# A long convolution with a gated layer: the third transform stage with 64 moving columns, real and imaginary parts kept apart, mirrored places joined by sum and difference; one late tap moved

## The chip, the core and the metric

The kernel runs on one core of a Trainium2 chip. The core has TensorE (matrix products into PSUM; PE in the profile, with PEld for its weight loads), VectorE (DVE), ScalarE (ACT), GpSimd (POOL), and SyncE (SP), whose queue issues all transfers here. Each engine works through its own instructions in program order and waits on semaphores for the others. The metric is the device time of one execution in microseconds (us).

## What is computed

For eight sequences of 6400 places and 128 channels, a causal convolution with one filter as long as the sequence is followed by a small gated layer:

```python
Xf = rfft(x, n=2*S, axis=1); Hf = rfft(h, n=2*S, axis=0)
x = irfft(Xf * Hf, n=2*S, axis=1)[:, :S]
gate = sigmoid(sum_k conv_w[k] * shifted(x, K - 1 - k))      # K = 5 taps, per channel
out = (gate * (x @ w_val)) @ w_out
```

All numbers are float32, in and out. x is (8, 6400, 128), h is (6400, 128), w_val and w_out are 128 x 128.

## The kernel before

The long transform is done as matrix products. The 6400 places are a 100 x 64 grid (N1 = 100, N2 = 64), so a transform along the sequence becomes a product of length 100, one of length 64 with twiddle factors, a product with the filter's spectrum, and the same way back. For one batch there are four stages:

- The **forward** half (`Forward.half`): 16 calls of four channels pairs each; products of 50 rows by 100 columns, into PSUM, copied to `gy` (two copies of 400 elements, both on ScalarE). Its inputs `sd` are sums and differences that POOL makes from the loaded tiles `x` (two per call).
- **Second stage with the filter** (`Product`): products with `m2`, multiplied by the spectrum `h` on VectorE, added on POOL, back into `gy`.
- **Third stage** (`s3_quads`): 16 calls a batch, each for eight channels, from `gy` into `dt` (seen as `dv[p, n, c, d]`: place n of 64, part c real or imaginary, channel d).
- **Fourth stage** (`Chunk.s4`): from `dt` and the tables `m4` to the result of the convolution, in 13 chunks of four or five places n, followed by the taps, the value product (`project`), the sigmoid, the gate product on VectorE, the output product and the store.

Work of different batches is laid over each other by the main loop at the end of the function `longconv_moe`. For each batch b a first inner loop runs 16 steps g: the third stage of batch b (`s3_quads(4 * g)`), and beside it the forward half of batch b + 1 (if there is one). I call these 16 steps the third stage of a batch. A second inner loop then runs the fourth stage of batch b beside the second stage of batch b + 1. Five chunks of the fourth stage (places 35 to 59, `late`) leave their taps, value product, sigmoid and gate for the 16 steps of the next batch: the list `steps` gives late chunk m its first two taps in step 2m, the others in step 2m + 1, value product, sigmoid and gate in step 2m + 2, and for the first three chunks the output product in step 2m + 4 and the store in 2m + 5. So steps 0 to 9 carry taps; steps 10 to 15 carry only the rest of the last late chunk and a chunk called HEAD.

`_Engines` keeps every instruction of an engine in program order, so an instruction that waits holds back all behind it on that engine.

**The third stage in detail** (lines 331 to 351). A call has 32 matmuls: four channels q, two halves c of the sum, four combinations of row half r and channel half k. Weights are slices of `gy` (64 by 64, or 64 by 50 for the second half c), the moving operand is a row of `r3_sb` with 128 columns: 64 places times real and imaginary part, interleaved. The two halves c add up in PSUM (start at c == 0, stop at c == 1). A float32 matmul is two matmul instructions and two weight loads. The result lies in two single PSUM banks (`single()`, of four) and is copied to `dt` by two copies of 512 elements, the first on ScalarE, the second on VectorE (on ScalarE in the last batch). The forward half writes into a pair of banks (`pair()`, of two pairs here).

**The taps** (lines 396 to 450). A chunk adds its result, weighted, to the cells of five neighbours. `first(4, ...)` on ScalarE initialises a cell (`init`); `more(j, ...)` on VectorE adds tap j. For chunks that are not late the fourth tap (j = 3) is made by `first(3, ...)` on ScalarE into a buffer `p_t` and added by POOL; for late chunks all of j = 0, 1, 2, 3 are `more` on VectorE.

Of the kernel before, what the change touches and what calls it, by code (L numbers as in the profile page):

```python
# [16 lines left out]
C = 128  # L17
N1 = 100
# [35 lines left out]
def _constants():  # L54
    k1 = np.arange(N1, dtype=np.float64)
    n1 = np.arange(N1, dtype=np.float64)
    k2 = np.arange(N2, dtype=np.float64)
    n2 = np.arange(N2, dtype=np.float64)
    half = np.arange(2 * HP) % HP
    own = half < HR  # L60
    tau = 2.0 * np.pi
    a = tau * np.outer(half + 0.5, k1 + 0.25) / N1
    r1 = np.stack([np.cos(a) + np.sin(a), np.cos(a) - np.sin(a)], axis=1) * own[:, None, None]
    al = tau * (
        (k1[None, :, None] + 0.25) * n2[:, None, None] / N
        + np.outer(n2, k2)[:, None, :] / N2
        - (k1[None, :, None] + 0.25) / (2 * N1)
    )
# [7 lines left out]
    r3 = []  # L76
    for p in range(2):
        b = tau * np.outer(k2 + p / 2, n2) / N2
        c, d = np.cos(b), np.sin(b)
        g = 1 - 2 * p  # L80
        r3.append(np.stack([np.stack([c, -g * d], -1), np.stack([-d, -g * c], -1)], 1))
    r3 = np.concatenate(r3, axis=0)
    t = N2 * n1[None, :] + np.arange(N2 + 1)[:, None]
    sign = np.where(np.arange(2 * HP)[:, None] < HP, 1.0, 1 - 2 * (n1 % 2))
    m4 = np.cos(tau * (half[:, None, None] + 0.25) * t[None] / N) / N * own[:, None, None] * sign[:, None]
    m4 = np.concatenate([m4[:, :, ::2], m4[:, :, 1::2], -m4[:, :, 1::2]], axis=2)
# [25 lines left out]
def longconv_moe(ctx: ExitStack, tc: tile.TileContext, x, h, r1, m2, r3, m4, w64, out):  # L112
# [7 lines left out]
    psp = tc.tile_pool(name="psp", bufs=2, space=bass.MemoryType.PSUM)  # L120
    pairs = [ps2, psp.__enter__()]

    gy = cp.tile([128, C // 2, N1, 2], F32, name="gy")
    dt = cp.tile([128, N2 * 2 * C], F32, name="dt")
    dv = dt.rearrange("p (n c d) -> p n c d", c=2, d=C)
    gh = dt[:, : N1 * C].rearrange("p (d k t) -> p d k t", k=N1, t=2)
    m4_sb = cp.tile([128, N2 + 1, MW], F32, name="m4_sb")
    r1_sb = cp.tile([128, 2, N1], F32, name="r1_sb")
    r3_sb = cp.tile([128, 2, 2 * N2], F32, name="r3_sb")
    w_sb = cp.tile([C, NW], F32, name="w_sb")  # L130
    wc_sb = w_sb[:, 2 * C :]
    gl = cp.tile([128, N2 - LATE, N1], F32, name="gl")
# [78 lines left out]
    class Forward:  # L211
# [19 lines left out]
            e.tensor_tensor(out=sd[:, 0], in0=x[:, 0], in1=x[:, 1], op=ADD)  # L231
            self.load()

        def half(self):
            j = self.i
            self.i += 1
            sd = sd_sb[(j + self.o) % 3]
            pt = pair()
            for m in range(XG):
                for r, c in ((0, 0), (1, 1), (1, 0), (0, 1)):  # L240
                    rows = slice(r * HP, r * HP + HR)
                    nc.tensor.matmul(
                        pt[c * N2 : (c + 1) * N2, r, m * N1 : (m + 1) * N1],
                        lhsT=sd[rows, c, m, :],
                        rhs=r1_sb[rows, c, :],
                        start=True,
                        stop=True,
                    )
            v = pt[:, :, : XG * N1].rearrange("p r (d t k) -> p r d k t", t=2, k=N1)
            d0 = j * XG // 2  # L250
            return [
                lambda e, r=r: e(self.dst[:, r * C // 4 + d0 : r * C // 4 + d0 + XG // 2], v[:, r]) for r in range(2)
            ]

    def count(kb):
# [73 lines left out]
                e.tensor_tensor(out=self.u[:, c], in0=self.u[:, c], in1=self.t[:, 1 - c], op=op)  # L329

    def s3_quads(d0):
        pts = [single(), single()]
        for q in range(4):
            for c in range(2):
                for r, k in ((0, 0), (1, 0), (1, 1), (0, 1)):
                    d, o = k * HP + d0 + q, (r + k) % 2
                    m = HR if c else HP
                    nc.tensor.matmul(
                        pts[k][o * HP : o * HP + m, q * 2 * N2 : (q + 1) * 2 * N2],
                        lhsT=gy[r * HP : (r + 1) * HP, d // 2, c * HR : c * HR + m, d % 2],  # L340
                        rhs=r3_sb[r * HP : (r + 1) * HP, c, :],
                        start=c == 0,
                        stop=c == 1,
                    )
        return [
            lambda e, k=k: e(
                dv[:, :, :, k * HP + d0 : k * HP + d0 + 4].rearrange("p n c d -> p (n c) d"),
                pts[k].rearrange("p (d m) -> p m d", d=4),
            )
            for k in range(2)  # L350
        ]

    def m4v(n, c, k):
        v = m4_sb[:, N2 - n if c else n, :].rearrange("p (b m) -> p b m", m=HR)
        if c:
            return v[:, 1::-1, ::-1] if not k else v[:, ::-2, ::-1]
        return v[:, 0:2, :] if not k else v[:, ::2, :]

    def cells(x, n):

# [10 lines left out]
    class Chunk:  # L371
# [8 lines left out]
        def s4(self):  # L380
            a, n = self.ch
            pt = single()
            for q in range(n):
                for c in range(2):
                    for k in range(2):
                        o = slice(k * HP, (k + 1) * HP)
                        nc.tensor.matmul(
                            pt[o, q * N1 : (q + 1) * N1].rearrange("p (m b) -> p b m", b=2),
                            lhsT=dv[:, a + q, c, o],
                            rhs=m4v(a + q, c, k),  # L390
                            start=c == 0,
                            stop=c == 1,
                        )
# [34 lines left out]
        def taps(self, js=range(4)):  # L428
            a, n = self.ch
            if self.late and 0 in js:  # L430
                self.init()
            if a == HEAD[0]:
                for j in range(1, 4):
                    for i, o in cells(a + j, n - j):
# [77 lines left out]
    nc.sync.dma_start(r3_sb, r3)  # L512

    def m4_load(j):
        a = slice(CH * j, CH * j + CH)
# [27 lines left out]
    for b in range(B):  # L543
# [16 lines left out]
        for g in range(NS):  # L560
            e = s3_quads(4 * g)
            f = []
            if nxt:
                f = fx.half()
                fx.sums(nc.gpsimd)
            e[0](act)
            e[1](dve if nxt else act)
            for u in f:
                u(act)
            if b == 0:  # L570
                next(wgen, None)
                next(wgen, None)
# [107 lines left out]
```

## Time and profile before

| What | us |
|---|---|
| Median of three runs (lowest, highest) | 997.13 (994.02, 997.45) |
| The profiled execution's own time | 994.58 |
| Its span, from first to last instruction | 992.7 |
| Third stage of batch 2, to the first matmul of its fourth stage | 53.5 |
| Fourth stage of batch 2 | 59.5 |

The profile is of one execution. Its page gives the busy time of each engine, the chain of work that ended last, the groups of like instructions, and the DMA queues. A group's row reads: engine, operation, tile written and tiles read, shape, count, then total busy time and mean duration (ns) of one, then the idle time of the engine just before them and what ended it. Nearly all instructions are recorded at line 99, the helper that keeps program order, so groups are told apart by tiles and shapes: `pt<-r_sb,gy` is the third stage, `pt<-r_sb,sd` the forward half, `pt<-m_sb,dt` the fourth stage, `pt<-gy,m` the second, `dt<-pt` copies or taps, `sd<-x` POOL's sums. A row of the timeline reads: start, duration (of the merged instructions), engine, what, count, and in brackets the idle time before it with what ended it; "issue" is an engine that waited for nothing the profile shows. A row of the windows reads: stretch, its length, then each engine's busy time with its count, the clock granted to TensorE, the DMA engines' mean busy share and the rate in GB/s. Some matmul records can be missing from a trace.

### The profile page before, as it was taken

The page shows a single profiled execution, that of the slowest core. Times are in us where ns is not written, and L with a number is a line of the kernel's source. Part 1 is how long each engine was busy: PE and PEld are TensorE (multiplying, and loading weights), DVE is VectorE, ACT ScalarE, POOL GpSimd, SP SyncE. Part 2 cuts the span into 40 slices and gives each one's busy share as a digit, 9 for nine tenths or more (in the row PEclk, how much of TensorE's full clock was granted, in tenths as well). Part 3 has the DMA queues.
Part 4 walks back from the last instruction along what each step waited for, and adds up shares of the span by engine and source line. Part 5 has one row for each costly group of instructions (what it writes and reads, how often), then busy time and mean ns, then how long its engine had stood idle before and what let it go on. Part 6 is the DMA issues. An engine that isn't in the chain of part 4 may idle for free.

```text
span 992.7 us, 47023 instructions
## 1 busy us (share of the span) xinstructions
PE 936.5 (94%) x21360; PEld 818.4 (82%) x21360; DVE 685.2 (69%) x923; ACT 488.3 (49%) x932; POOL 544.6 (55%) x551
## 2 busy tenths in 40 slices
PE   7798879999999999999899999999999999999978
PEld 6698879888899879997799878998787888996854
DVE  4557437968299656967499665978489674976366
ACT  4522435536444554536444554536544464536656
POOL 5557534785177743786267842776367852760032
PEclk8999899999999999999999999999999999999989
DMA  7785545955387554855378563865478563850103
GB/s 242 249 293 206 187 168 202 277 135 192 100 265 199 172 194 138 246 167 174 121 245 221 151 200 122 259 167 183 139 242 222 142 206 110 265 144 24 42 23 112
DMA packets 96839, 177.35 MB, mean 179 GB/s; under 512 B 43392, under 2 KB 49792, under 8 KB 96640
## 3 DMA queue, kind: packets, MB, share of 16 engines
q1 hardware_dynamic: 96640, 174.34, 56.3%
q8 instruction: 168, 2.75, 1.1%
q14 instruction: 31, 0.25, 0.1%
HBM read 141.55 MB, written 32.77 MB: 176 GB/s over the span
## 4 chain that ended last, share of the span: by engine, by line
PE 88%; issue 4%; DMA 3%; DVE 2%; POOL 2%; ACT 1%; SPq 0%; DVEq 0%; POOLq 0%
PE pt L99 88%; DMA x<-xl 3%; DVE gl L99 1%; POOL sd L99 1%; ACT dt L99 1%; DVE dt L99 1%; POOL dt L99 0%; DMA x<-hl 0%; SPq L99 0%; POOL gl L99 0%; DVE gy L99 0%; DVE m_sb L99 0%; DVE sd L99 0%; ACT yl L99 0%; ACT gy L99 0%
## 5 line engine op out<-in xcount | busy, mean ns | idle before, releaser
L99 ACT COPY dt<-pt 128x512 f32<-128x512 f32 (+3 forms) x285 | 163.1, 582 | 251.9 <-PE pt L99 250.5
L99 PE MATMUL pt<-r_sb,gy 64*50 64x128 f32 (+1 forms) x8192 | 266.3, 274 | 21.4 <-issue 15.8
L99 POOL TENSOR_TENSOR gy<-gy,h 128x512 f32<-128x512 f32 (+1 forms) x182 | 221.1, 1240 | 117.9 <-PE pt L99 81.9
L99 PEld LDWEIGHTS pt<-r_sb,gy 64*50 64x50 f32 (+1 forms) x8192 | 235.8, 130 | 60.3 <-issue 26.6
L99 POOL TENSOR_TENSOR sd<-x 128x256 f32<-128x256 f32 x236 | 199.2, 869 | 143.6 <-issue 112.4
L99 PEld LDWEIGHTS pt<-m_sb,dt 128*64 128x64 f32 x4096 | 203.8, 137 | 30.0 <-issue 14.7
L99 PE MATMUL pt<-m_sb,dt 128*64 128x100 f32 x4096 | 205.6, 250 | 4.8 <-DVE dt L99 4.0
L99 PEld LDWEIGHTS pt<-gy,m 128*64 128x64 f32 x3008 | 192.7, 135 | 17.6 <-issue 5.3
L99 PE MATMUL pt<-gy,m 128*64 128x128 f32 x3008 | 199.7, 277 | 0.6 <-PE pt L99 0.5
L99 PE MATMUL pt<-r_sb,sd 50*64 50x100 f32 x4608 | 143.9, 258 | 23.6 <-issue 13.6
L99 DVE COPY dt<-pt 128x512 f32<-128x512 f32 (+1 forms) x120 | 81.4, 679 | 122.4 <-PE pt L99 109.9
L99 DVE TENSOR_TENSOR gy<-pt,h 128x1024 f32<-128x1024 f32 (+1 forms) x99 | 116.9, 1181 | 52.7 <-PE pt L99 26.5
L99 PEld LDWEIGHTS pt<-r_sb,sd 50*64 50x64 f32 x4608 | 128.2, 141 | 30.1 <-issue 16.7
L99 DVE SCALAR_TENSOR_TENSOR gl<-yl,w_sb,gl 128x500 f32<-128x500 f32 x147 | 127.5, 872 | 23.1 <-ACT gl L99 20.4
L99 DVE SCALAR_TENSOR_TENSOR dt<-pt,w_sb,dt 128x500 f32<-128x500 f32 (+7 forms) x216 | 132.6, 630 | 11.7 <-POOL dt L99 5.2
L99 ACT COPY gy<-pt 128x400 f32<-128x400 f32 x248 | 110.1, 496 | 45.8 <-PE pt L99 38.0
L99 PE MATMUL pt<-dt,w_sb 128*64 128x500 f32 (+2 forms) x480 | 126.2, 560 | 2.3 <-ACT dt L99 1.8
L99 DVE TENSOR_TENSOR h<-pt,h 128x1024 f32<-128x1024 f32 (+1 forms) x91 | 107.7, 1184 | 3.5
L99 ACT COPY yl<-pt 128x500 f32<-128x500 f32 (+1 forms) x89 | 51.0, 573 | 90.7 <-PE pt L99 90.6
L99 POOL TENSOR_TENSOR dt<-dt,p 128x500 f32<-128x500 f32 (+1 forms) x64 | 66.3, 1041 | 23.4 <-PE pt L99 12.7
L99 DVE TENSOR_TENSOR gl<-pt,gl 128x500 f32<-128x500 f32 (+1 forms) x48 | 31.5, 660 | 59.6 <-PE pt L99 33.2
L99 ACT ACTIVATE dt<-dt 128x500 f32<-128x500 f32 (+1 forms) x64 | 36.5, 571 | 66.5 <-POOL dt L99 66.1
(41 smaller groups left out, 588.2 us busy)
## 6 DMA issues: line engine op xcount, KB each, us to landing
m<-m SPq DMA_DIRECT2D x90, 512.0 KB, 5.3
h<-hd SPq DMA_DIRECT2D x84, 512.0 KB, 5.4
x<-xl SPq DMA_DIRECT2D x118, 256.0 KB, 2.9
out<-dt SPq DMA_DIRECT2D x56, 250.0 KB, 4.4
out<-yl SPq DMA_DIRECT2D x40, 250.0 KB, 2.6
m_sb<-m SPq DMA_DIRECT2D x13, 375.0 KB, 6.8
hd<-h SPq DMA_DIRECT2D x8, 512.0 KB, 4.7
m_sb<-m SPq DMA_DIRECT2D x6, 512.0 KB, 7.0
```

The lines of the kernel that those rows point to most:

```text
L99: return self._tc.keep_in_program_order(call(*args, **kwargs))
```

## The change

In the third stage the real and imaginary parts are no longer made for all 64 places. The two halves c of the sum are kept apart instead of added up in PSUM: each matmul has 64 moving columns (32 places for each of two parts), starts and stops by itself, and writes every second PSUM column. A call has as many matmuls as before. The results of places n and 64 - n are then the sum and the difference of the two halves, formed on the way out of PSUM. All weights are 64 by 64 now; the slices of the second half c run past their channel, so `gy` gets a zeroed tail, and the surplus rows meet zeros in `m4`. The third stage writes a pair of banks (`pair()`), the forward half two singles. The evacuation is four pieces: `keep` (ScalarE copies one half, 512 elements, to a scratch tile, half of `h_sb[HB - 1]`, used in turn), two `join`s (VectorE, sum and difference of PSUM and scratch, 496 elements each), and `ends` (ScalarE, two copies of 16 elements for places 0 and 32). In a step they come in the order keep, join, join, the forward half's two copies, ends. The upper places hold real and imaginary parts exchanged, which `m4` (with one row more) and `m4v` make good. The spectrum tile whose buffer is the scratch is loaded after the 16 steps. Apart from this, the fourth tap (j = 3) of late chunks is done as in the other chunks: `first(3, ...)` on ScalarE into `p_t`, added by POOL.

The changes in `_constants` (tables computed on the host's side) are left out, save the third stage's:

```diff
@@ _constants
     for p in range(2):
-        b = tau * np.outer(k2 + p / 2, n2) / N2
+        b = tau * np.outer(k2 + p / 2, n2[: N2 // 2]) / N2
         c, d = np.cos(b), np.sin(b)
-        g = 1 - 2 * p
-        r3.append(np.stack([np.stack([c, -g * d], -1), np.stack([-d, -g * c], -1)], 1))
+        q, r = -d, -d
+        q[:, 0], r[:, 0] = alt, -alt
+        r3.append(np.stack([np.concatenate([c, q], 1), np.concatenate([-c, r], 1)], 1))
...
@@ longconv_moe
-    gy = cp.tile([128, C // 2, N1, 2], F32, name="gy")
+    gyf = cp.tile([128, C * N1 + 2 * (HP - HR) + 4], F32, name="gy")
+    gy = gyf[:, : C * N1].rearrange("p (d k t) -> p d k t", k=N1, t=2)
+    nc.vector.memset(gyf[:, C * N1 :], 0.0)
...
-    m4_sb = cp.tile([128, N2 + 1, MW], F32, name="m4_sb")
+    m4_sb = cp.tile([128, N2 + 2, MW], F32, name="m4_sb")
...
-    r3_sb = cp.tile([128, 2, 2 * N2], F32, name="r3_sb")
+    r3_sb = cp.tile([128, 2, N2], F32, name="r3_sb")
...
@@ Forward.half
-        def half(self):
+        def half(self, pt=None):
...
-            pt = pair()
+            if pt is None:
+                pt = pair()
+                pt = [pt[:, 0], pt[:, 1]]
...
@@ s3_quads
-        pts = [single(), single()]
+        pt = pair()
         for q in range(4):
             for c in range(2):
                 for r, k in ((0, 0), (1, 0), (1, 1), (0, 1)):
                     d, o = k * HP + d0 + q, (r + k) % 2
-                    m = HR if c else HP
+                    w = d // 2 * 2 * N1 + c * 2 * HR + d % 2
+                    v = pt[o * HP : (o + 1) * HP, k, q * 2 * N2 : (q + 1) * 2 * N2].rearrange("p (b m) -> p b m", b=2)
                     nc.tensor.matmul(
-                        pts[k][o * HP : o * HP + m, q * 2 * N2 : (q + 1) * 2 * N2],
-                        lhsT=gy[r * HP : (r + 1) * HP, d // 2, c * HR : c * HR + m, d % 2],
+                        v[:, :, c::2],
+                        lhsT=gyf[r * HP : (r + 1) * HP, w : w + 2 * HP - 1 : 2],
                         rhs=r3_sb[r * HP : (r + 1) * HP, c, :],
-                        start=c == 0,
-                        stop=c == 1,
+                        start=True,
+                        stop=True,
                     )
-        return [
-            lambda e, k=k: e(
-                dv[:, :, :, k * HP + d0 : k * HP + d0 + 4].rearrange("p n c d -> p (n c) d"),
-                pts[k].rearrange("p (d m) -> p m d", d=4),
+        v = pt.rearrange("p k (d b m) -> p b m k d", b=2, m=N2)
+        a = d0 // 4 % 2 * 512
+        t = h_sb[HB - 1][:, a : a + 512]
+        o = dv.rearrange("p n c (k d) -> p (n c) k d", k=2)[:, :, :, d0 : d0 + 4]
+
+        def keep():
+            act(
+                t.rearrange("p (d m c) -> p d m c", m=N2 // 2, c=2)[:, :, :, ::-1],
+                pt.rearrange("p k (d b m c) -> p b (k d) m c", b=2, m=N2 // 2, c=2)[:, 1],
             )
-            for k in range(2)
-        ]
+
+        def join(op, n):
+            u = t.rearrange("p (k d m) -> p m k d", k=2, d=4)
+            nc.vector.tensor_tensor(out=n, in0=v[:, 0, 2:], in1=u[:, 2:], op=op)
+
+        def ends():
+            act(o[:, 0:2], v[:, 0, :2])
+            act(o[:, N2 : N2 + 2], v[:, 1, :2])
+
+        return keep, lambda: join(ADD, o[:, 2:N2]), lambda: join(ALU.subtract, o[:, : N2 + 1 : -1]), ends
...
@@ Chunk.taps
             if self.late and 0 in js:
                 self.init()
+                self.q = p_t[a // CH % 2]
+                self.first(3, self.q, self.p)
...
             for j in js:
-                if j < 3 or self.late:
+                if j < 3:
                     for i, o in cells(a + j, n):
                         self.more(j, o, self.p[:, i : i + o.shape[1]])
-            if self.late:
+            if 3 not in js:
                 return
             for i, o in cells(a + 3, n):
                 nc.gpsimd.tensor_tensor(out=o, in0=o, in1=self.q[:, i : i + o.shape[1]], op=ADD)
...
@@ main loop, the 16 steps
             if nxt:
-                f = fx.half()
+                f = fx.half([single(), single()])
                 fx.sums(nc.gpsimd)
-            e[0](act)
-            e[1](dve if nxt else act)
+            for u in e[:3]:
+                u()
             for u in f:
                 u(act)
+            e[3]()
...
-                else:
+                elif kb < M2B + HB - 1:
                     h_load(kb - M2B)
             for u in steps[g]:
                 u()
+        if nxt:
+            h_load(HB - 1)
```

More of the change, by code (lines that the diff above doesn't have):

```diff
@@ L76, in _constants @@
     r3 = []
+    alt = 1.0 - 2.0 * (k2 % 2)
     for p in range(2):
-        b = tau * np.outer(k2 + p / 2, n2) / N2
+        b = tau * np.outer(k2 + p / 2, n2[: N2 // 2]) / N2
         c, d = np.cos(b), np.sin(b)
-        g = 1 - 2 * p
-        r3.append(np.stack([np.stack([c, -g * d], -1), np.stack([-d, -g * c], -1)], 1))
+        q, r = -d, -d
+        q[:, 0], r[:, 0] = alt, -alt
+        r3.append(np.stack([np.concatenate([c, q], 1), np.concatenate([-c, r], 1)], 1))
     r3 = np.concatenate(r3, axis=0)
     t = N2 * n1[None, :] + np.arange(N2 + 1)[:, None]
-    sign = np.where(np.arange(2 * HP)[:, None] < HP, 1.0, 1 - 2 * (n1 % 2))
-    m4 = np.cos(tau * (half[:, None, None] + 0.25) * t[None] / N) / N * own[:, None, None] * sign[:, None]
-    m4 = np.concatenate([m4[:, :, ::2], m4[:, :, 1::2], -m4[:, :, 1::2]], axis=2)
+    up = np.arange(2 * HP)[:, None, None] >= HP
+    base = np.cos(tau * (half[:, None, None] + 0.25) * t[None] / N) / N * own[:, None, None]
+    flip = base * (1 - 2 * (n1 % 2))
+    m4 = np.where(up, flip, base)
+    m4[HP:, N2 // 2 + 1 :] *= -1
+    mid, odd = base[:, N2 // 2 : N2 // 2 + 1], flip[:, N2 // 2 : N2 // 2 + 1, ::-1]
+    m4[:, N2 // 2] = np.where(up, odd, mid)[:, 0]
+    m4 = np.concatenate([m4, np.where(up, mid, odd)], axis=1)
+    ev, od = m4[:, :, ::2], m4[:, :, 1::2]
+    late = ((np.arange(N2 + 2) > N2 // 2) & (np.arange(N2 + 2) <= N2))[None, :, None]
+    m4 = np.concatenate([np.where(late, od, ev), np.where(late, ev, od), np.where(late, -ev, -od)], axis=2)
     f = lambda v: np.ascontiguousarray(v.astype(np.float32))
@@ L242, in half @@
                     nc.tensor.matmul(
-                        pt[c * N2 : (c + 1) * N2, r, m * N1 : (m + 1) * N1],
+                        pt[r][c * N2 : (c + 1) * N2, m * N1 : (m + 1) * N1],
                         lhsT=sd[rows, c, m, :],
@@ L248, in half @@
                     )
-            v = pt[:, :, : XG * N1].rearrange("p r (d t k) -> p r d k t", t=2, k=N1)
+            v = [p[:, : XG * N1].rearrange("p (d t k) -> p d k t", t=2, k=N1) for p in pt]
             d0 = j * XG // 2
             return [
-                lambda e, r=r: e(self.dst[:, r * C // 4 + d0 : r * C // 4 + d0 + XG // 2], v[:, r]) for r in range(2)
+                lambda e, r=r: e(self.dst[:, r * C // 4 + d0 : r * C // 4 + d0 + XG // 2], v[r]) for r in range(2)
             ]
@@ L341, in s3_quads @@
                         rhs=r3_sb[r * HP : (r + 1) * HP, c, :],
-                        start=c == 0,
-                        stop=c == 1,
-                    )
-        return [
-            lambda e, k=k: e(
-                dv[:, :, :, k * HP + d0 : k * HP + d0 + 4].rearrange("p n c d -> p (n c) d"),
-                pts[k].rearrange("p (d m) -> p m d", d=4),
-            )
-            for k in range(2)
-        ]
-    def m4v(n, c, k):
[L354 to L357, printed above, removed]
+                        start=True,
@@ new lines, in join @@
+        def join(op, n):
[5 more added lines that the diff above has]
+        return keep, lambda: join(ADD, o[:, 2:N2]), lambda: join(ALU.subtract, o[:, : N2 + 1 : -1]), ends
+    def m4v(n, c, k):
+        e = N2 - n if c else n
+        if n == N2 // 2:
+            v = m4_sb[:, N2 + 1 if k else n]
+        else:
+            v = m4_sb[:, e]
+        v = v.rearrange("p (b m) -> p b m", m=HR)
+        w = v[:, :, ::-1] if c else v
+        if c == (e > N2 // 2):
+            return w[:, ::2] if k and n != N2 // 2 else w[:, 0:2]
+        return w[:, ::-2] if k and n != N2 // 2 else w[:, 1::-1]
@@ L388, in s4 @@
                             pt[o, q * N1 : (q + 1) * N1].rearrange("p (m b) -> p b m", b=2),
-                            lhsT=dv[:, a + q, c, o],
+                            lhsT=dv[:, a + q, 1 - c if a + q > N2 // 2 else c, o],
                             rhs=m4v(a + q, c, k),
@@ L514, in m4_load @@
     def m4_load(j):
-        a = slice(CH * j, CH * j + CH)
+        a = slice(CH * j, CH * j + CH + (j == 12))
         nc.sync.dma_start(m4_sb[:, a], m4.rearrange("k (n t) -> k n t", t=MW)[:, a])
```

## The prediction

> **What bounds the kernel now.** I read the page first, then the stretches of the stages (busy time of each engine in windows), then the timeline inside them, then the waits.
>
> ```profile
> PE 936.5 (94%) x21360; PEld 818.4 (82%) x21360; DVE 685.2 (69%) x923; ACT 488.3 (49%) x932; POOL 544.6 (55%) x551
> ...
> PE 88%; issue 4%; DMA 3%; DVE 2%; POOL 2%; ACT 1%; SPq 0%; DVEq 0%; POOLq 0%
> ...
> q8 instruction: 168, 2.75, 1.1%
> ```
>
> TensorE is busy for 94% and makes 88% of the chain that ended last, so a change that halves moving columns looks like a change on the path. That average hides the stages:
>
> ```profile
> core 0: us, PE busy (x) PEld busy (x) DVE busy (x) ACT busy (x) POOL busy (x), PEclk, DMA share, GB/s
> 98.30:153.00 54.70, 44.99 (x1519) 43.08 (x1523) 20.57 (x38) 22.24 (x46) 24.31 (x33) 0.91 0.49 161
> 326.50:380.00 53.50, 50.67 (x1573) 42.25 (x1572) 32.04 (x43) 30.29 (x61) 27.58 (x32) 1.00 0.51 160
> ...
> 890.90:931.90 41.00, 38.94 (x1061) 30.56 (x1060) 18.96 (x27) 24.67 (x47) 0.00 (x0) 1.00 0.07 23
> ```
>
> The rows are the third stage of batch 0, of batch 2 (I take it for 1 to 6) and of batch 7, which has no forward transform beside it. Only these change; the fourth stage between them keeps its work. How long does TensorE really need in one step?
>
> ```profile
> 826.29 1.98 PE L99 MATMUL pt<-r_sb,gy 64*64 64x128 f32 x64
> 828.09 0.87 PE L99 MATMUL pt<-r_sb,sd 50*64 50x100 f32 x32
> 828.78 1.93 PE L99 MATMUL pt<-r_sb,gy 64*64 64x128 f32 x64
> ...
> 890.85 5.47 PE L99 MATMUL pt<-r_sb,gy 64*64 64x128 f32 x192
> ```
>
> A step (64 matmul instructions of the third stage, 32 of the forward transform; each f32 matmul is two) goes from start to start in 828.78 - 826.29 = 2.49 us: 1.73 for the third stage (5.47 less a tail of 0.27, over three calls), 0.7 for the other. Sixteen steps are 39.8 us. Batch 0 has nothing else on TensorE and takes 54.7. Where the 15 us go:
>
> ```profile
> 138.76 0.97 PE L99 MATMUL pt<-r_sb,gy 64*64 64x128 f32 x27
> 142.92 0.92 PE L99 MATMUL pt<-r_sb,gy 64*50 64x128 f32 x12 [3.19 <-issue]
> ...
> PEld pt L99 <- issue: 9.5, 6, 3.4
> PE pt L99 <- issue: 8.2, 5, 3.2
> ```
>
> The first two rows are batch 0's timeline, the others its waits (us, times, longest). In the middle of a call TensorE stands still for 3.19 us and waits for no engine. The instruction queue of the page explains it: 168 packets for 2 x 21360 instructions, 254 in each. A step has 192, so the stage needs twelve packets, one every 54.7 / 12 = 4.6 us, and that, not the columns, is its length. I read it so: the next packet is asked for late, and under DMA load it takes some 4.6 us. The change leaves the count of instructions as it is.
>
> **The change part by part.**
>
> ```profile
> L99 PE MATMUL pt<-m_sb,dt 128*64 128x100 f32 x4096 | 205.6, 250 | 4.8 <-DVE dt L99 4.0 <-ACT dt L99 0.7
> ...
> L99 PE MATMUL pt<-r_sb,sd 50*64 50x100 f32 x4608 | 143.9, 258 | 23.6 <-issue 13.6 <-DVE sd L99 5.0 <-POOL sd L99 3.9
> ```
>
> Matmuls: same number, 64 columns for 128. Rounds of four go in 1.73 / 16 = 0.108 us at 128 columns and 0.7 / 8 = 0.087 at 100, so 64 columns should take 0.054 (in proportion) to 0.061 (on that line): some 0.93 us a call, 0.8 less, 13 us a stage. The other bound is no gain, if weight loads or the write of every second PSUM column limit it. The fourth stage writes every second column already (row one) and takes 250 ns at 100 columns where a contiguous write takes 258, so I take 0.93. The Trainium skill's "PSUM — Partial Sum Buffer", section Specifications, says that a non-contiguous pattern slows matmuls significantly; by it the call would stay at 1.73, which is rival 3.
>
> Evacuation, per step. It was one copy on ScalarE and one on VectorE. Now it is keep (512 elements, ScalarE), two joins (496 each, VectorE), then ends (two copies of 16, ScalarE).
>
> ```profile
> L99 ACT COPY dt<-pt 128x512 f32<-128x512 f32 x145 | 83.3, 586 | 149.8 <-PE pt L99 148.5 <-DMA x<-xl 1.4
> ...
> L99 ACT COPY gy<-pt 128x400 f32<-128x400 f32 x248 | 110.1, 496 | 45.8 <-PE pt L99 38.0
> ...
> L99 DVE COPY dt<-pt 128x512 f32<-128x512 f32 x112 | 76.9, 686 | 113.9 <-PE pt L99 109.9 <-DMA x<-xl 4.0
> ...
> L99 DVE TENSOR_TENSOR gl<-pt,gl 128x500 f32<-128x500 f32 x40 | 27.0, 678 | 45.7 <-PE pt L99 33.2 <-ACT gl L99 11.3
> ...
> 346.15 0.89 ACT L99 COPY gy<-pt 128x400 f32<-128x400 f32 x2
> ```
>
> VectorE: minus 0.69, plus 2 x 0.68. ScalarE: the copies of 400 and 512 give 0.8 ns an element over 0.175, so an end is 0.19; two copies of 0.496 take 0.89 together, so each overlaps its neighbour by 0.1, and both ends hold ScalarE for 0.18.
>
> The order costs more than the sums. Keep, joins and ends read the same two PSUM banks. Does a reader on ScalarE wait for a reader on VectorE? Before shows the pair the other way round, in the last batch:
>
> ```profile
> 937.72 0.68 ACT L99 ACTIVATE dt<-pt,w_sb 128x500 f32<-128x500 f32 x1
> ...
> 938.29 0.68 ACT L99 ACTIVATE p<-pt,w_sb 128x500 f32<-128x500 f32 x1
> ...
> 939.06 2.40 DVE L99 SCALAR_TENSOR_TENSOR dt<-pt,w_sb,dt 128x400 f32<-128x400 f32 x6 [0.38 <-ACT p L99]
> ...
> DVE dt L99 <- ACT p L99: 3.4, 3, 1.7
> ```
>
> VectorE's tap reads PSUM and dt, not p, yet starts 0.09 us after the ACTIVATE that fills p from the same bank, though dt was ready since 938.40. So readers of one bank go one after another, and I take 0.09 as the price of a hand-over. Then **ends waits for both joins, and behind ends, in order on ScalarE, stand the sigmoid, the initial tap, the new fourth tap, the store copy and the next keep**; the next joins, gate and taps on VectorE wait for those. A plain step is at least 0.59 + 0.09 + 0.68 + 0.68 + 0.09 + 0.18 = 2.3 us. The forward copies fit under the joins and cost nothing as long as TensorE is ahead.
>
> The fourth late tap: one of four taps goes from VectorE to an ACTIVATE and an add on POOL.
>
> ```profile
> L99 DVE SCALAR_TENSOR_TENSOR gl<-yl,w_sb,gl 128x500 f32<-128x500 f32 x140 | 123.7, 884 | 23.1 <-ACT gl L99 20.4
> ...
> L99 ACT ACTIVATE gl<-gl 128x500 f32<-128x500 f32 x40 | 25.1, 630 | 10.6 <-DVE gl L99 9.5 <-POOL gl L99 0.9
> ...
> L99 ACT ACTIVATE gl<-yl,w_sb 128x500 f32<-128x500 f32 x28 | 19.8, 708 | 0.0
> ...
> L99 POOL TENSOR_TENSOR gl<-gl,p 128x500 f32<-128x500 f32 x5 | 6.2, 1247 | 13.0 <-DVE gl L99 13.0
> ...
> L99 POOL TENSOR_TENSOR sd<-x 128x256 f32<-128x256 f32 x236 | 199.2, 869 | 143.6 <-issue 112.4
> ```
>
> A late chunk takes two steps. Even step, from the start of its keep: keep to 0.59, joins to 2.04, ends from 2.13, sigmoid of the chunk before 2.3 to 2.93, initial tap to 3.54, fourth tap (taken at 0.7) to 4.14. VectorE: gate 3.02 to 3.70, two taps to 5.47. Odd step: keep (from 4.04) is long done, joins 5.47 to 6.83, ends from 6.92, store copy 7.1 to 7.68, the next keep at 7.58; tap three to 7.71. **So 7.6 us a pair, 7.1 where nothing is stored.** POOL's add ends at 7.71 + 0.09 + 1.25 = 9.05, before the next sigmoid wants it (7.58 + 2.3): hidden. POOL's sums queued behind it are two steps ahead, and POOL has 4 x 0.87 + 1.25 = 4.7 us of work in 7.6. What the pair took before:
>
> ```profile
> 345.91 2.01 PE L99 MATMUL pt<-r_sb,gy 64*64 64x128 f32 x61
> ...
> 352.97 0.49 PE L99 MATMUL pt<-r_sb,gy 64*64 64x128 f32 x7
> ...
> 902.99 2.19 PE L99 MATMUL pt<-r_sb,gy 64*64 64x128 f32 x68
> ...
> 909.37 0.34 PE L99 MATMUL pt<-r_sb,gy 64*64 64x128 f32 x4
> ```
>
> 7.06 with the forward transform, 6.38 without. Pairs of the new stage: 6.5 (no gate yet), 7.1, 7.6, 7.6, 8.2 (the last late chunk has one short tap more), then for the steps with no taps 5.3 (gate at 3.70, joins and ends behind it), 5.1 and 4.7 (two plain steps, in one a sigmoid): 52.1, and 1.1 to the first keep, 53.2.
>
> Batch 7: 53.2, less 1.2 because its taps run without POOL beside them: 52 against 41.0, **plus 11**. There TensorE's 13 us are no help: its steps with no taps took 1.73 and take 2.3.
>
> Batches 1 to 6: 53.2, plus 1.0 for the first step (the forward copies stand before ends and wait for POOL's first sums), 54.2. Steps 10 to 15 count 15.1 in that; their 1152 instructions are 4.5 packets, up to 20 us at 4.6, but TensorE now comes there a step ahead; I add 1.0 of a possible 0 to 3. 55.2 against 53.5: plus 1.7, between -1 and +3.5, **six times: plus 10**.
>
> Batch 0: bound by packets before and after; the end gains the wait of the fourth stage for the last joins and ends (2.3 where the forward matmuls covered 0.7), less 0.8 of the last call: **plus 1** (-1 to +2).
>
> At nothing: one m4 row and 32 padding elements more; one h load moved behind the stage, on SP ahead of loads that are due later, wanted three steps later.
>
> Sum: 1 + 10 + 11 = 22 us on the profiled execution's 994.6 us (span 992.7): 1017. The median of the runs, 997.1, would give 1019.
>
> **Rivals.** 1. **Ends does not wait for the joins** (reads are ordered only where I saw it). Then ScalarE runs ahead and VectorE decides: 4 x 0.68 + 0.68 + 3 x 0.88 = 6.05 a pair, and 0.8 idle before the gate (add, sigmoid), 6.85 against 7.06; batches 1 to 6 gain 2 each, batch 7 loses 2: 985, faster. It decides as soon as ends starts within 0.2 us of the forward copies. For it: no data connects ends and joins. Against: the 0.38 us row.
> 2. **Packets do not bind the new stage**: then batch 0 goes by plain steps, 16 x 2.3 + 1 = 38, 18 less than forecast, and the 1.0 in each of six batches goes: 993, no change. For it: TensorE is idle in only 2.8 of the 53.5 us of batch 2. Against: the 3.19 us row, where TensorE had 2.49 us of work a step and will have 1.6. The Trainium skill stands on this side: "Runtime: NRT & Kernel Launch", section Instruction fetch mechanics, holds the refill in 16 KiB blocks to be hidden behind the issue of instructions.
> 3. **The matmuls gain nothing** (columns written two apart, or weight loads): 1.73 a call, TensorE is no step ahead, packets and chain add up, 2 to 3 us more in each of six: 1032.
> 4. **TensorE's time is the time**: 13 us in each of eight stages, 890. Against it: 32 joins of 0.68 alone are 21.8 us on VectorE where 11 went, and the packets.
>
> **How the numbers follow.** Forecast 0.70 (996 to 1031 from the bounds of the three terms), rival 1 0.10, rival 2 0.12, rival 3 0.06, rival 4 0.02. A measurement of this kernel tells some 0.5% (5 us) from no change. Faster is 1 and 4, 0.12; same is 2, 0.12; slower the rest, 0.76. The range takes the forecast and rival 2: 990 to 1033.
>
> **What would show it.** Right: ends starting 0.1 us behind the second join; VectorE idle before gates until ScalarE's gl; pairs of 7.1 to 7.6; the third stage of batch 7 near 52 us; batch 0 near 55 with TensorE idle "by issue"; a third-stage call in 0.9 to 1.0 us. Wrong: ends beside a join (rival 1); a call of 1.7 us (rival 3); batch 0 well under 50 (no packet limit); taps on VectorE far from 0.88.

## The result, and the profile after

The changed kernel takes 1063.31 us (median of 4 runs, 1059.4 to 1063.72) where the kernel before took 995.88 us beside it (994.02 to 997.45): a ratio of 1.0669, 95% interval 1.0635 to 1.0703. Slower, as forecast, but by 67 us and not by 22; the time lies 30 us above the range. Here and below a ratio compares runs in the chip's faster state only, with runs of the kernel before taken beside them.

The page of the changed kernel: busy time of each engine, the instruction queue, and the groups that answer to the evacuation.

```profile
PE 883.4 (84%) x21360; PEld 717.9 (68%) x21360; DVE 822.6 (78%) x1033; ACT 511.8 (48%) x1207; POOL 558.1 (53%) x586
...
q8 instruction: 168, 2.75, 1.1%
...
L109 DVE TENSOR_TENSOR dt<-pt,h 128x496 f32<-128x496 f32 x256 | 250.8, 1022 | 71.1 <-ACT h L109 59.1
```

The number of TensorE's instructions and of its packets is the same, and its busy time fell by 53 us. VectorE's rose by 137. The last row carries most of the result: **a join takes 1.02 us**, where the prediction took 0.68. 256 joins are 251 us of VectorE; at 0.68 they would be 174.

The windows of the changed kernel: busy time (and number) of PE, PEld, DVE, ACT, POOL, then granted clock, DMA share and GB/s. The rows are the third stage of batch 0, the third and the fourth stage of batch 2, and the third stage of batch 7.

```profile
core 0: us, PE busy (x) PEld busy (x) DVE busy (x) ACT busy (x) POOL busy (x), PEclk, DMA share, GB/s
96.70:150.28 53.58, 36.76 (x1536) 34.47 (x1537) 41.12 (x55) 25.96 (x79) 24.18 (x33) 0.84 0.48 156
331.90:391.85 59.95, 43.43 (x1574) 32.22 (x1573) 47.20 (x54) 35.16 (x100) 28.88 (x37) 0.96 0.41 133
391.85:453.60 61.75, 61.75 (x986) 52.58 (x987) 51.20 (x66) 25.81 (x49) 40.47 (x36) 0.96 0.71 209
938.30:995.94 57.64, 35.64 (x1064) 23.69 (x1061) 44.93 (x54) 22.27 (x67) 6.27 (x5) 0.78 0.05 16
```

Against the rows of before: batch 0 is 1 us shorter (54.70 to 53.58; the row of before stops 0.6 us short of the first fourth-stage matmul, up to which it is 55.3), batch 2 6.5 longer, batch 7 16.6 longer. The fourth stage, which the prediction left alone, is longer too. Its row before, in the same columns:

```profile
380.00:439.50 59.50, 59.50 (x992) 55.31 (x988) 51.33 (x67) 26.57 (x49) 40.47 (x36) 1.00 0.70 208
```

61.75 against 59.50, with the granted clock at 0.96 instead of 1.00. I cut the whole trace at the first matmul of each third and each fourth stage. The differences in span (1057.4 against 992.7):

| | forecast | changed kernel |
|---|---|---|
| third stage, batch 0 | +1 | -1.6 |
| third stages, batches 1 to 6 | +10 | +40.6 |
| third stage, batch 7 | +11 | +16.5 |
| eight fourth stages | 0 | +10.8 |
| ahead of the first third stage | 0 | -1.7 |

How a step goes shows in the timeline of batch 2, cut to the rows on the path (start, length, engine, operation, in square brackets the idle time before and what ended it):

```profile
341.10 0.60 ACT L109 COPY h<-pt 128x512 f32<-128x512 f32 x1
...
341.74 2.01 DVE L109 TENSOR_TENSOR dt<-pt,h 128x496 f32<-128x496 f32 x2 [0.15 <-ACT h L109]
...
343.78 0.25 ACT L109 COPY dt<-pt 128x16 f32<-128x16 f32 x2 [1.28 <-DVE dt L109]
343.92 0.63 ACT L109 ACTIVATE gl<-gl 128x500 f32<-128x500 f32 x1
...
344.58 0.68 DVE L109 TENSOR_TENSOR gl<-pt,gl 128x500 f32<-128x500 f32 x1 [0.83 <-ACT gl L109]
...
345.18 1.88 DVE L109 SCALAR_TENSOR_TENSOR gl<-yl,w_sb,gl 128x500 f32<-128x500 f32 x2
...
346.98 1.94 DVE L109 TENSOR_TENSOR dt<-pt,h 128x496 f32<-128x496 f32 x2
...
348.95 0.25 ACT L109 COPY dt<-pt 128x16 f32<-128x16 f32 x2 [1.94 <-DVE dt L109]
349.08 0.60 ACT L109 COPY h<-pt 128x512 f32<-128x512 f32 x1
```

This is the chain that the prediction wrote down: keep, two joins, ends within 0.1 us of the second join (341.74 + 2.01 = 343.75, then 343.78), the sigmoid behind ends, VectorE idle for 0.83 us until ScalarE has it, the gate, two taps, two joins, a tap that falls beside ends, the next keep. From keep to keep the pair takes 7.98 us where 7.1 was forecast (nothing is stored in this one): the two spans from joins to ends are 2.04 and 1.97 us instead of 1.45 each, 1.1 together, and the rest is 0.2 shorter.

### The profile page after: what moved, and what is told of

It reads as the page before. It is cut to its first block, busy times and chain, and to the rows that moved or that the text cites. A ratio compares the mean times of both kernels' runs of the same rounds, so it can differ in the third digit from the quotient of the medians.

```text
span 1057.4 us, 47726 instructions
## 1 busy us (share of the span) xinstructions
PE 883.4 (84%) x21360; PEld 717.9 (68%) x21360; DVE 822.6 (78%) x1033; ACT 511.8 (48%) x1207; POOL 558.1 (53%) x586
## 5 line engine op out<-in xcount | busy, mean ns | idle before, releaser
L109 DVE TENSOR_TENSOR dt<-pt,h 128x496 f32<-128x496 f32 x256 | 250.8, 1022 | 71.1 <-ACT h L109 59.1
L109 ACT COPY dt<-pt 128x16 f32<-128x16 f32 (+3 forms) x397 | 112.1, 319 | 286.1 <-DVE dt L109 183.1
L109 PEld LDWEIGHTS pt<-r_sb,gy 64*64 64x64 f32 x8192 | 149.9, 142 | 120.2 <-ACT dt L109 84.9
L109 PE MATMUL pt<-r_sb,gy 64*64 64x64 f32 x8192 | 168.4, 231 | 71.9 <-ACT dt L109 54.0
L109 PEld LDWEIGHTS pt<-gy,m 128*64 128x64 f32 x3008 | 182.0, 137 | 29.1 <-issue 24.9
L109 PE MATMUL pt<-r_sb,sd 50*64 50x100 f32 x4608 | 153.5, 259 | 54.7 <-issue 22.8
L109 POOL TENSOR_TENSOR sd<-x 128x256 f32<-128x256 f32 x236 | 170.1, 752 | 38.7 <-issue 15.9
L109 POOL TENSOR_TENSOR gl<-gl,p 128x500 f32<-128x500 f32 (+1 forms) x48 | 56.9, 1185 | 166.4 <-ACT yl L109 96.5
L109 DVE SCALAR_TENSOR_TENSOR dt<-pt,w_sb,dt 128x500 f32<-128x500 f32 (+7 forms) x216 | 132.6, 630 | 10.7 <-POOL dt L109 6.7
L109 PE MATMUL pt<-dt,w_sb 128*64 128x500 f32 (+2 forms) x480 | 114.5, 555 | 2.3 <-ACT dt L109 1.8
L109 ACT COPY h<-pt 128x512 f32<-128x512 f32 (+1 forms) x136 | 84.5, 622 | 35.6 <-PE pt L109 34.9
L109 DVE SCALAR_TENSOR_TENSOR gl<-yl,w_sb,gl 128x500 f32<-128x500 f32 (+1 forms) x112 | 89.9, 808 | 11.8 <-POOL sd L109 7.0
```

Source lines behind the costliest of these rows:

```text
L109: return self._tc.keep_in_program_order(call(*args, **kwargs))
```

## The experiments

### Is it the length of the join, and what makes it long?

In the changed kernel the scratch `t` lies in the order channel half, channel, place (k, d, m), and the joins walk it in the order place, half, channel: successive elements are 64 elements, 256 bytes, apart. The first experiment puts the scratch into the joins' own order. Keep still walks it in its old order, so now its writes have the gaps.

```diff
 keep:
-                t.rearrange("p (d m c) -> p d m c", m=N2 // 2, c=2)[:, :, :, ::-1],
+                t.rearrange("p (m c d) -> p d m c", m=N2 // 2, c=2)[:, :, :, ::-1],
 join:
-            u = t.rearrange("p (k d m) -> p m k d", k=2, d=4)
+            u = t.rearrange("p (m k d) -> p m k d", k=2, d=4)
```

> The changed kernel with the scratch laid out in the order in which the joins read it (places, then channels), so that a join's second input lies without gaps and keep writes with gaps instead. Theory (a join takes 1.02 us and not 0.68 because successive elements of its scratch input lie 64 elements apart): joins 0.67 to 0.70 us, keep no dearer than 0.70, a pair of steps with taps 7.1 to 7.4 us where it was 8.0, a step without taps 2.3 where it was 2.7; the whole 995 to 1025 us where the changed kernel has 1063. Rival (PSUM read in steps of 512 bytes beside any SBUF input, or the short runs of the output, make it slow): joins stay at 1.0 us, the whole at 1055 to 1070.

Measured: 1033.02 us, ratio 1.0415 (1.0362 to 1.0469). The groups of this run (busy time, mean ns of one, idle time before):

```profile
L109 DVE TENSOR_TENSOR dt<-pt,h 128x496 f32<-128x496 f32 x256 | 160.6, 669 | 127.1 <-ACT h L109 126.3
...
L109 ACT COPY h<-pt 128x512 f32<-128x512 f32 x128 | 150.4, 1175 | 18.2 <-PE pt L109 18.2
```

The joins fall from 1022 to 669 ns, as the theory said. It missed what keep would do: 1175 ns for 597, for the gaps have moved into ScalarE's writes, and VectorE now waits 126 us for keep (59 before). So the total came down by 30 us and not by the 38 and more that were expected.

The next kernel makes keep walk the scratch in the joins' order too. The gaps that are left are in the reads of PSUM.

```diff
 keep:
-                t.rearrange("p (m c d) -> p d m c", m=N2 // 2, c=2)[:, :, :, ::-1],
-                pt.rearrange("p k (d b m c) -> p b (k d) m c", b=2, m=N2 // 2, c=2)[:, 1],
+                t.rearrange("p (m c d) -> p m c d", m=N2 // 2, c=2)[:, :, ::-1],
+                pt.rearrange("p k (d b m c) -> p b m c (k d)", b=2, m=N2 // 2, c=2)[:, 1],
```

> The changed kernel with the scratch in the joins' order, as in the run e1, and keep also going through its elements in that order, so that neither touches SBUF with gaps between successive elements; PSUM alone is read in steps of 128 elements, as the copies before the change did. Theory (gaps in SBUF make the access slow, on either engine; steps in PSUM cost nothing): keep 0.58 to 0.62 us, joins 0.67, the stages as the forecast had them (about 55 us in batches 1 to 6, 52 in batch 7), the whole 1008 to 1025. Rival (the extra time sits in reordering 512 elements, wherever it is done): keep stays near 1.17, the whole near 1033.

Measured: 1005.3 us, ratio 1.0084 (1.0053 to 1.0116), a little under the expected 1008. Its groups, then its windows (third stage of batches 0 and 2, fourth stage of batch 2, third stage of batch 7):

```profile
L109 DVE TENSOR_TENSOR dt<-pt,h 128x496 f32<-128x496 f32 x256 | 160.2, 667 | 98.5 <-ACT h L109 98.5
...
L109 ACT COPY h<-pt 128x512 f32<-128x512 f32 x128 | 76.3, 596 | 38.0 <-PE pt L109 37.3 <-POOL sd L109 0.6
```

```profile
97.27:151.27 54.00, 36.15 (x1537) 34.03 (x1537) 30.12 (x55) 26.23 (x80) 23.96 (x33) 0.85 0.49 155
324.07:377.88 53.81, 42.75 (x1574) 31.49 (x1573) 37.48 (x54) 34.87 (x98) 30.58 (x37) 0.97 0.47 148
377.88:437.20 59.32, 59.32 (x985) 50.87 (x985) 51.20 (x66) 26.23 (x51) 40.44 (x36) 1.00 0.75 217
895.50:942.47 46.97, 30.90 (x1064) 21.46 (x1061) 34.27 (x54) 22.28 (x67) 6.25 (x5) 0.93 0.06 20
```

Two access patterns, with nothing else changed, take 58 us of the 67 away. Both instructions are now short (667 and 596 ns), though both read PSUM in steps of 128 elements: gaps in PSUM cost nothing here, gaps in the scratch, which lies in SBUF, cost 0.35 us a join or 0.58 us a keep. This is the kernel that the prediction priced, since its joins and its keep have the durations of the sum: against before its third stages are at -1.3 (batch 0), +7.9 (batches 1 to 6 together) and +5.9 us (batch 7), its fourth stages at +0.1.

The Trainium skill has this rule, and the prediction did not use it. Its page "SBUF — State Buffer", section "Door 1: The DMA port swizzle", says that SBUF gives full bandwidth within a line of 16 bytes and takes a penalty for each new line, so that float32 can be walked for free only in steps of up to four. The two rows of joins, 1022 and 667 ns, agree. The same passage says of PSUM, with lines of 8 bytes, that access with gaps slows matmuls; the matmuls of the changed kernel, which write every second column, show none of it (below).

### Is it the place of ends?

Ends reads the same two banks as the joins, and the prediction said that it waits for them and holds back all of ScalarE. The edit puts it right behind keep:

```diff
-            for u in e[:3]:
+            for u in (e[0], e[3], e[1], e[2]):
                 u()
             for u in f:
                 u(act)
-            e[3]()
```

> The changed kernel with ends issued right after keep, ahead of both joins, nothing else. Theory (readers of the same banks go one after another, and ends behind the joins holds ScalarE up, with the sigmoid, the initial taps and the next keep behind it): ScalarE no longer waits for VectorE in a step, a pair with taps goes by VectorE's own work, 4 x 0.95 + 0.68 + 3 x 0.82 = 6.9 us, where it was 8.0, and a step without taps by two joins, 1.95, or by the packets of instructions; the whole 1025 to 1045 us. Rival (VectorE's sum binds already, and the wait of ends costs nothing): the whole within 6 us of 1063.

Measured: 1033.95 us, ratio 1.0405 (1.0355 to 1.0456), with joins as long as in the changed kernel. The group of ends in the changed kernel, and then in this one:

```profile
L109 ACT COPY dt<-pt 128x16 f32<-128x16 f32 x256 | 31.7, 177 | 183.1 <-DVE dt L109 183.1
```

```profile
L109 ACT COPY dt<-pt 128x16 f32<-128x16 f32 x256 | 33.9, 195 | 0.0
```

ScalarE stood idle before ends for 183.1 us, all of it released by VectorE; here it does not wait at all, and the time falls by 29 us. The same edit on the kernel with short joins:

> The run e8 with ends issued right after keep, ahead of the joins. Theory (two separate costs, slow joins and the hold-up of ScalarE, so the gains add up): batches 1 to 6 at the packets' 50 to 53 us, batch 7 at 42 to 45, the whole 985 to 1003. Rival (they overlap, and once the joins are fast the order of ends is worth nothing): within 5 us of e8.

Measured: 1001.97 us (8 runs, 994.27 to 1012.66), ratio 1.0027 (1.0 to 1.0055): 3 us better than without it, which the two intervals do not separate. It is the best version of the change by its median, and it does not beat the kernel before. The total fits the theory and the rival alike; the stages tell more. In batch 7 the order is worth 4.5 us (46.94 to 42.44), as the theory said; batches 1 to 6 went from 55.0 to 54.4 on average, where 50 to 53 was expected, and the fourth stages lost 3.3 us in all, since two more of them began at half clock. Why so little? TensorE's waits (us in total, times, longest) in the changed kernel, then in this one:

```profile
PE pt L109 <- ACT dt L109: 55.8, 52, 3.1
PE pt L109 <- issue: 38.8, 35, 3.2
```

```profile
PE pt L109 <- issue: 64.5, 46, 3.2
PE pt L109 <- DVE dt L109: 22.8, 24, 2.7
```

In the changed kernel TensorE waits most for the evacuation, here for nothing that the profile shows, "issue". As the evacuation gets shorter, that wait takes its place.

### What bounds the third stage before: columns or instructions?

Two edits on the kernel before. Both halve the columns that TensorE has to stream; the first keeps the number of matmuls, the second halves it and keeps 128 columns in each (left out here: the copies of the first, which read its 64 columns twice, and start and stop of the second, both now True):

```diff
 half the columns:
-                        pts[k][o * HP : o * HP + m, q * 2 * N2 : (q + 1) * 2 * N2],
+                        pts[k][o * HP : o * HP + m, q * 2 * N2 : q * 2 * N2 + N2],
-                        rhs=r3_sb[r * HP : (r + 1) * HP, c, :],
+                        rhs=r3_sb[r * HP : (r + 1) * HP, c, :N2],
...
 half the instructions:
-            for c in range(2):
+            for c in range(1):
...
```

> The kernel before with 64 moving columns in the third stage and the copies as they were in size and number (each reads the 64 columns twice, so the output is not the reference's: half of the places of the third stage are left out and filled with the other half). The count of TensorE's instructions is unchanged. Theory (packets of instructions bind the third stage): batch 0's stage stays at 52 to 55 us, the whole at 970 to 995. Rival (TensorE's time is the time): 13 us less in each of eight stages, 890 to 905.

> The kernel before with only the first half of the sum in the third stage: 16 matmuls of 128 columns a call where it has 32, the copies unchanged (the second half of the sum is left out, so the output is not the reference's). The columns streamed are those of the run with half the columns, the instructions of a step 128 where there 192. Theory (packets): batch 0's stage 36 to 42 us, the whole 905 to 935, some 60 us below the run with half the columns. Rival (columns count, instructions do not): the same as the run with half the columns within 6 us.

Measured: 973.52 us with half the columns, ratio 0.9795 (0.9731 to 0.986); 914.16 us with half the instructions, ratio 0.9198 (0.9152 to 0.9245). The windows, third stage of batch 0 and of batch 7, for half the columns and then for half the instructions, with the instruction queue of the latter:

```profile
99.70:152.54 52.84, 36.98 (x1536) 35.07 (x1536) 20.82 (x39) 22.61 (x46) 24.20 (x33) 0.81 0.51 167
874.50:906.80 32.30, 27.46 (x1061) 19.14 (x1060) 18.99 (x27) 24.51 (x47) 0.00 (x0) 1.00 0.08 29
```

```profile
97.73:139.10 41.37, 32.71 (x1024) 31.09 (x1024) 21.60 (x39) 22.07 (x46) 24.39 (x33) 0.84 0.63 211
818.30:849.72 31.42, 27.09 (x550) 17.25 (x549) 19.00 (x27) 24.34 (x47) 0.00 (x0) 1.00 0.08 27
```

```profile
q8 instruction: 136, 2.23, 1.0%
```

In batch 0 (55.3 us before, cut in the same way), with DMA traffic beside it, half the columns give 2.4 us and half the instructions 13.9. In batch 7, with next to no traffic (DMA share 0.08), both give about the same, 8.7 and 9.6 us. TensorE's waits go with this: with half the columns, 13.3 us of them are by "issue" in batch 0 and none in batch 7, where 4.0 us are for VectorE and ScalarE. So beside the loads the third stage is bound by the arrival of TensorE's instructions: 32 packets fewer are four a stage, and 13.9 us for four packets is 3.5 us each. The DMA rows of the instruction queue, for batch 0 before and for batch 7 with half the columns:

```profile
q8 instruction: 12, 0.20, 1.4%
```

```profile
q8 instruction: 9, 0.15, 1.8%
```

1.4% of 16 engines for 54.7 us, over twelve packets, is 1.0 us each, and 1.8% for 32.3 us, over nine, is 1.0 as well: a packet travels no longer with the loads than without. In the trace of before, each of the five waits by "issue" in batch 0 ends 1.3 to 1.4 us behind the landing of a packet, so these waits are for packets that come late. What makes them late, no run here shows.

The change halves columns only. What it could win was therefore 2 to 3 us a stage in batches 0 to 6 (half the columns: 2.4 us in batch 0, 2.8 on average in the others) before anything was paid for the evacuation.

### The fourth late tap

In the changed kernel the move is undone; in the kernel before it is made alone, by the same lines the other way round:

```diff
 Chunk.taps, on the changed kernel:
                 self.init()
-                self.q = p_t[a // CH % 2]
-                self.first(3, self.q, self.p)
...
-                if j < 3:
+                if j < 3 or self.late:
...
-            if 3 not in js:
+            if self.late:
                 return
```

> The changed kernel with the fourth late tap back on VectorE. Theory (VectorE decides the steps with taps): each of five pairs in seven stages longer by 0.4 to 0.7 us, the whole 1073 to 1090. Rival (the tap's ACTIVATE on ScalarE, which is held up anyway, costs as much as it frees on VectorE): within 6 us of 1063.

> The kernel before with only the fourth late tap moved to ScalarE and POOL. Theory (before, TensorE and its packets set the length of the steps with taps, VectorE has room): no change, 989 to 1000, at most 1 us in any stage. Rival (the sigmoid waits for POOL's add, later than for the tap on VectorE): 0.5 us in each of 35 pairs, 1005 to 1015.

Measured: 1077.27 us, ratio 1.0801 (1.0752 to 1.085), 14 us worse than with the move; and 998.62 us, ratio 0.9997 (0.9968 to 1.0027), no difference. The move pays where VectorE is on the path, as it is with the long joins, and nothing where it is not.

### Why are the fourth stages longer?

The timeline of the changed kernel at the end of the third stage of batch 2: the last forward matmuls, the last joins, the last ends, and the first fourth-stage matmuls. Behind it TensorE's row of the kernel before at the same place.

```profile
389.57 0.40 PE L109 MATMUL pt<-r_sb,sd 50*64 50x100 f32 x6 [1.54 <-issue]
...
389.80 1.90 DVE L109 TENSOR_TENSOR dt<-pt,h 128x496 f32<-128x496 f32 x2 [0.80 <-ACT h L109]
...
391.73 0.25 ACT L109 COPY dt<-pt 128x16 f32<-128x16 f32 x2 [0.83 <-DVE dt L109]
...
391.85 2.93 PE L109 MATMUL pt<-m_sb,dt 128*64 128x100 f32 x32 [1.88 <-DVE dt L109]
```

```profile
380.01 1.67 PE L99 MATMUL pt<-m_sb,dt 128*64 128x100 f32 x31
```

TensorE stands still for 1.54 us by "issue", works for 0.40, stands still for another 1.88 us until the last joins and ends are through, and then its first 32 matmuls take 2.93 us where 31 took 1.67. To see whether the idle time makes them slow, four matmuls of constants by constants, into a bank that nobody reads, fill it:

```diff
         if nxt:
             h_load(HB - 1)
+        pt = single()
+        for q in range(4):
+            nc.tensor.matmul(
+                pt,
+                lhsT=r3_sb.rearrange("p c n -> p (c n)"),
+                rhs=m4_sb[:, :N2].rearrange("p n t -> p (n t)")[:, 512 * q : 512 * q + 512],
+                start=True,
+                stop=True,
+            )
```

> The changed kernel with four more f32 matmuls of 128x512 (constants by constants, into a bank that nobody reads) on TensorE behind the last third-stage call of each batch, in the 1.9 to 4.2 us in which it stood idle before the fourth stage. Theory: the 1 to 2.8 us by which the first 64 fourth-stage matmuls are later in the changed kernel's trace (9.2 to 10.7 us instead of 7.9) come from a clock that drops when TensorE idles; with the filler they take 7.9 to 8.2 us again, the fourth stages are 59.3 to 59.6 us (before: 59.5), and the total falls by 6 to 10 us, to 1053 to 1057. Rival: the fourth stages are longer because VectorE and ScalarE are behind by then; the filler changes nothing (1061 to 1065), or delays the stage by its own length (1068 and more).

Measured: 1055.76 us, ratio 1.0613 (1.0581 to 1.0645). The timeline at the place, and the windows of the third and fourth stage of batch 2:

```profile
390.35 3.70 PE L109 MATMUL pt<-m_sb,r_sb 128*128 128x512 f32 x8
393.98 1.59 PE L109 MATMUL pt<-m_sb,dt 128*64 128x100 f32 x32
```

```profile
332.57:393.98 61.41, 45.74 (x1582) 32.24 (x1580) 47.25 (x54) 35.23 (x100) 28.92 (x37) 1.00 0.42 132
393.98:453.40 59.42, 59.42 (x989) 52.25 (x988) 51.21 (x66) 25.70 (x47) 40.47 (x36) 1.00 0.74 218
```

The 32 matmuls are back at 1.59 us, and the fourth stage at 59.42 with the clock at 1.00; cut in the same way, the eight fourth stages fall from 486.5 to 473.6 us. None of them begins at half clock, while in the changed kernel the clock is down at the beginning of seven of the eight, or falls within 1 us of it. The total falls by less, since the third stages, at whose end the filler stands, are longer in this trace (483.6 us in all against 474.2). By the totals alone the two intervals overlap a little; the rows carry the verdict. The Trainium skill, "TensorE: Matmul & The Clock Gate", section "Part 1: The HAM clock gate", says that TensorE's clock is halved after an idle window of some 3.4 us, and that the windows run freely. 2.93 against 1.59 us is nearly a factor of two and agrees. The idle time agrees less. The windows of the changed kernel around the place, cut where its granted clock changes:

```profile
386.60:390.01 3.41, 1.82 (x84) 1.43 (x75) 2.61 (x4) 1.95 (x6) 0.00 (x0) 1.00 0.02 5
390.01:396.84 6.83, 5.00 (x46) 4.22 (x48) 1.69 (x2) 1.82 (x6) 0.10 (x1) 0.50 0.25 79
396.84:400.25 3.41, 3.41 (x60) 3.33 (x58) 1.76 (x2) 1.17 (x3) 0.00 (x0) 1.00 0.44 109
```

The clock fell at 390.01 us, 0.04 us into the idle time of 1.88 us, so it was not this one alone that brought it down. It stayed at half for 6.83 us, which is two times 3.41, and all changes of the clock in this trace are whole multiples of 3.41 us apart, as windows that run freely would have it. But no window without work was needed: in the 3.41 us before the fall TensorE was busy for 1.82.

> The changed kernel with the scratch in the joins' order and kept in that order, ends ahead of the joins, and the same filler. Theory: its trace without the filler lost 1.6 us in two of eight fourth stages, so the filler is worth 0 to 4 us there: 997 to 1002, not measurably under the kernel before, because the third stages of batches 1 to 6 stay at 53 to 56 us (twelve packets of some 4.5 us). Rival: the third stage is bound by its evacuation and not by packets, and the filler, with its 8 more instructions, is seen as nothing: 1002, or worse by its own 3.5 us in each batch, 1025.

On the best version the same filler is a miss: 1013.43 us, ratio 1.0195 (1.0155 to 1.0234), against 1001.97 without. There TensorE's idle time before a fourth stage was 0.1 to 2.4 us, the filler takes 3.7, and what it delays is more than the clock gives back: in the two traces the fourth stages gain 5.5 us in all and the third stages lose 14.7.

## Why the prediction was right or wrong

**The direction was right, the size was not, and the step that failed is the price of the join: "VectorE: minus 0.69, plus 2 x 0.68".** The 0.68 came from the row of the gate product (678 ns), whose SBUF operand has no gaps; the join's has one behind each element. It measured 1.02 us. The prediction gave this price no second bound, so the range could not hold it. What the missing 0.34 us did, the comparison with the kernel with short joins shows: 10.7 us in batch 7 (32 joins of 0.355 us are 11.4), 33 us in batches 1 to 6, and the loss of clock in the fourth stages.

**Batches 1 to 6** were forecast at 55.2 us. With joins as priced they are 55.0 on average (330.2 / 6); with joins of 1.02 us they are 60.5 (363.0 / 6). That 55.0 meets 55.2 is in part luck. With short joins the four pairs behind the first, which carry taps, take 7.0 to 7.7 us in batch 2, from keep to keep, and the sum has 7.1 to 8.2; the plain step takes some 2.1 and the sum has 2.3 (with long joins it takes 2.8). Against that the pair of steps 12 and 13 takes 6.2 to 10.2 us in batches 1 to 6, where the sum has 5.1 and batch 7 takes 4.6. In batch 2 TensorE waits there for 1.70 us by "issue". So the allowance of 1.0 us for packets was too small by about 2, which the shorter pairs and steps made up.

**Batch 7**, forecast at 52, is 57.64, and 46.97 with joins as priced. Here the sum was 5 us too high. Its plain steps of 2.3 us take 2.1, and its taps of 0.88 us, of which it took off 1.2 us in all, take 0.74, with no sums of POOL beside them. The two taps behind a gate take, in the kernel with short joins, in batch 2 and in batch 7:

```profile
335.79 2.30 DVE L109 SCALAR_TENSOR_TENSOR gl<-yl,w_sb,gl 128x500 f32<-128x500 f32 x2
...
905.86 1.51 DVE L109 SCALAR_TENSOR_TENSOR gl<-yl,w_sb,gl 128x500 f32<-128x500 f32 x2
```

Over a stage's sixteen taps that is 3.2 us less than in batch 2, and over 2 us less than at the price of 0.88. In the total the 5 us hid part of the error of the joins.

**Batch 0**, "bound by packets before and after", held: 53.58 us for the forecast 55. Half the columns left it at 52.84, half the instructions took it to 41.37. Rival 2 (packets do not bind) is refuted by that, and with it, for this kernel, the rule of the Trainium skill that the prediction set beside it ("Runtime: NRT & Kernel Launch", section Instruction fetch mechanics): here the refill is not hidden. The prediction's reading that a packet takes some 4.6 us under load held only in part: it is on its way for 1.0 us, with the loads as without, and eight packets at 4.6 us would make 37 us and not 41.

**Ends waiting for the joins** was right to 0.1 us, and rival 1 is refuted by 183.1 us of idle time. "The order costs more than the sums" was wrong, though, with joins as priced: without that order the short joins still give 1001.97 instead of 1005.3; TensorE's waits by "issue" are behind it. Its 29 us exist only beside the long joins.

**A call** goes in 0.9 us, as forecast; rival 3 (matmuls gain nothing) is refuted. In the third stage of batch 2 of the changed kernel:

```profile
358.69 1.19 PE L109 MATMUL pt<-r_sb,gy 64*64 64x64 f32 x64
...
360.55 1.19 PE L109 MATMUL pt<-r_sb,gy 64*64 64x64 f32 x64
```

1.19 less the tail of 0.27 is 0.92. Rival 4 fell with the rest: TensorE's time was not the time.

**The fourth stage at nothing** was wrong by 10.8 us. The prediction saw that the fourth stage now waits for the last joins and ends, and counted 1.6 us for it in batch 0; it did not ask what the idle time does to TensorE's clock. **The fourth tap** hidden on ScalarE and POOL was right.

What stays open: in which cases an idle time lowers the clock. In the changed kernel it fell in batch 2 behind a window of 3.41 us in which TensorE was busy for 1.82 us. In batch 5 it stayed up through an idle time of 3.64 us, which lies in two windows with 1.74 and 1.45 us of work. So the busy time of a window alone does not tell it. Open too is why the packets come late beside the loads.

## What to carry to other kernels

Price an evacuation by the order in which it walks SBUF and not only by its number of elements, and let the instruction that fills a scratch write it in the order in which it is read; put the gaps on PSUM's side. Before halving the work of matmuls, ask whether their columns or the arrival of their instructions sets the pace: a stretch with DMA traffic and one without tell it apart, and so do TensorE's waits by "issue". And when TensorE gets ahead of the others, look at the clock of the stage that follows.

## What the runs showed that was not expected

- A VectorE instruction of 496 elements took 1.02 us with 256 bytes between the successive elements that it read from SBUF, and 0.67 us without; a ScalarE copy of 512 elements took 1.18 us with gaps in its writes to SBUF, and 0.60 without. Reads of PSUM with gaps cost neither of them anything.
- Filling 1.9 us of TensorE's idle time with useless matmuls made the stage behind it 2.3 us shorter (61.75 to 59.42), and the stage in front of it 1.5 us longer (59.95 to 61.41).
- Two VectorE taps of 500 elements took 2.30 us beside POOL's sums and 1.51 us without.
